# Query softmax of the next block, spread over the steps of a block

## The chip, the cores and the metric

The kernel runs on one core of a Trainium2 chip. The metric is the device time of one execution in microseconds, as the median of several runs. The core has TensorE (PE: matmuls; PEld: its weight loads), VectorE (DVE), ScalarE (ACT), GpSimd (POOL) and SyncE (SP), whose queue issues the DMAs. Each engine works through its own instructions in the order of the program and waits on semaphores for the others.

## What is computed

Attention over 49 agents, and two MLP layers without a residual. All is float32; there are 12480 tokens of 128 channels, and both MLPs have 2048 hidden units.

```python
def sm(a, b):
    s = (1/sqrt(128)) * (a @ b.T)
    s = s - s.max(-1, keepdims=True)
    e = np.exp(s)
    return e / (e.sum(-1, keepdims=True) + 1e-09)

agent_v = sm(agents, k) @ v            # 49 x 128
x = sm(q, agents) @ agent_v            # 12480 x 128
x = np.maximum(x @ w_in1, 0)**2 @ w_out1
h = x @ w_in2
return (np.maximum(h, 0) + alpha * np.minimum(h, 0)) @ w_out2
```

## The kernel before

The first part (up to about 120 us) reads k and v, makes the agents' attention and from it `agent_v`, and multiplies that with the first MLP's input weights once: W1 = agent_v @ w_in1. After that a query's softmax weights are all that the first layer needs. Every operand of these matmuls is split into a high and a low half (`...h`, `...l`), and a product is the sum of three matmuls, so an activation costs not only its ReLU but also a high copy and a subtraction for the low half.

The second part is one loop (line 748) over steps `s`. The 12480 queries are 25 blocks: one of 320 queries, 23 of 512, one of 384. A block is 8 steps (`b, i = divmod(s, 8)`), and a step handles 256 hidden units of both layers, of different blocks:

- `H1(s)`: first layer in, 6 matmuls into the PSUM tile `h1`; ScalarE does the ReLU (L647) and later the square (L757).
- `O(s - 2, ...)`: first layer out, 12 matmuls, from the halves `g1h` and `g1l` of step s - 2.
- `G1(s)`: VectorE makes `g1h` (L658) and `g1l` (L660); in a few steps of the first two blocks ScalarE or GpSimd does one of them.
- `H2(s - 11)`: second layer in, 12 matmuls into the PSUM tile `h2`; ScalarE makes `g2h` by a ReLU (L714), then VectorE makes `g2l` (L715), which reads `h2` too. There is one `h2`, so the next `H2` waits for `g2l`.
- `O2`: second layer out, 12 matmuls, one step behind `H2`.

At the end of a block come extra pieces: `X1_copy`, `X1_add` and `X1` (in step 1 of the next block: the first layer's result, its halves, `xl` on L694) and `OUT` (in step 3: copy on ScalarE, add and 32x32 transpose on VectorE, DMA).

Beside this the loop prepares the softmax of the next block's queries, mostly on VectorE. `q_transpose` (tile `qT`), `q_split_hi` on ScalarE and `q_split_lo` make the query's halves; `q_scores` is 12 narrow matmuls into `s_ps`, in the PSUM tile `h1`; `q_squares` transposes the scores back into the tile `s`. Each of the four groups of 32 partitions holds 25 agents (or 24 and a repeated one), so that two groups share a query. `q_max` reduces over 25, exchanges the results between the two groups (`swap`, four small copies on L282), takes the maximum of both (`m`) and subtracts it. `q_exp` is the exponential on ScalarE. `q_norm` sums, corrects for the repeated agent, exchanges, adds, takes the reciprocal and multiplies. `q_back` transposes back (`e2`, which shares the one buffer of `qT`), and `q_hi` and `q_lo` make the halves `qsh` and `qsl` for the next block's `H1`.

Which step does which is written by hand in two tables (lines 736 and 737). Entries of `before` come ahead of `H1` in a step's program, those of `after` at its end; the engines keep that order. The stretch from H1's first matmul to the next step's is called a step below, and step numbers are `i`.

Of the kernel before, what the change touches and what calls it, by code (L numbers as in the profile page):

```python
# [8 lines left out]
F32 = mybir.dt.float32  # L9
# [10 lines left out]
def agent_attention_moe_kernel(  # L20
# [43 lines left out]
    QB = 32  # L64
    NT = 512

    NQS = [10] + [NT // QB] * 23 + [12]
    assert sum(NQS) * QB == N
    Q0 = [sum(NQS[:b]) for b in range(len(NQS))]
    NB = len(NQS)  # L70
    H = 64
    GA = (NA + 1) // 2
# [13 lines left out]
    qp = ctx.enter_context(tc.tile_pool(name="qp", bufs=2))  # L86
# [82 lines left out]
    with tc.manual_schedule():  # L169
# [51 lines left out]
            return t_.rearrange("p r g a -> p (r g a)")  # L221


        q_sb, qh_sb, ql_sb, s2_ps, t_sb, e_sb, qs_sb = {}, {}, {}, {}, {}, {}, {}

        def flat(t_):
            return t_.rearrange("p j c -> p (j c)")
# [15 lines left out]
        def q_transpose(b):  # L243
            if b >= NB:
                return
            t_ = qp.tile([128, NT], F32, tag="qT", name="qT", bufs=1)[:, :QB * NQS[b]]
            nc.vector.transpose(t_, q_sb[b])
            q_sb[b] = t_

        def q_split_hi(b):  # L250
            if b >= NB:
                return
            qh_sb[b] = qp.tile([128, NT], F32R, tag="qh", name="qh", bufs=1)[:, :QB * NQS[b]]
            nc.scalar.copy(qh_sb[b], q_sb[b])

        def q_split_lo(b):
            if b >= NB:
                return
            ql_sb[b] = qp.tile([128, NT], F32R, tag="ql", name="ql", bufs=1)[:, :QB * NQS[b]]
            nc.vector.tensor_tensor(out=ql_sb[b], in0=q_sb.pop(b), in1=f32(qh_sb[b]), op=ALU.subtract)  # L260
# [17 lines left out]
        def swap(t_):  # L278

            for i in range(4):  # L280
                o = i ^ 1
                nc.vector.tensor_copy(t_[i * QB:(i + 1) * QB, 1, :], t_[o * QB:(o + 1) * QB, 0, :])  # L282
# [12 lines left out]
        def q_max(b):  # L295
            if b >= NB:
                return
            s = t_sb[b][:, :, :GA]
            mx = qp.tile([128, 2, NT // QB], F32, tag="mx", name="mx")[:, :, :NQS[b]]
            nc.vector.tensor_reduce(out=mx[:, 0, :], in_=s, op=ALU.max, axis=AX.X)  # L300
            swap(mx)
            m = qp.tile([128, NT // QB, 1], F32, tag="m", name="m")[:, :NQS[b]]
            nc.vector.tensor_tensor(out=m[:, :, 0], in0=mx[:, 0, :], in1=mx[:, 1, :], op=ALU.max)
            nc.vector.tensor_tensor(out=s, in0=s, in1=m.to_broadcast([128, NQS[b], GA]), op=ALU.subtract)  # L304

        def q_exp(b):
# [2 lines left out]
            s = t_sb[b][:, :, :GA]  # L309
            nc.scalar.activation(s, s, AF.Exp, scale=SCALE)  # L310

        def q_norm(b):
            if b >= NB:
                return
            s = t_sb[b][:, :, :GA]
            sm = qp.tile([128, 2, NT // QB], F32, tag="sm", name="sm")[:, :, :NQS[b]]
            nc.vector.tensor_reduce(out=sm[:, 0, :], in_=s, op=ALU.add, axis=AX.X)

            nc.vector.scalar_tensor_tensor(
                out=sm[:, 0, :], in0=s[:, :, GA - 1], scalar=notpad, in1=sm[:, 0, :], op0=ALU.mult, op1=ALU.add  # L320
            )
            swap(sm)
            r = qp.tile([128, NT // QB, 1], F32, tag="r", name="r")[:, :NQS[b]]
            nc.vector.scalar_tensor_tensor(
                out=r[:, :, 0], in0=sm[:, 0, :], scalar=1e-9, in1=sm[:, 1, :], op0=ALU.add, op1=ALU.add
            )
            nc.vector.reciprocal(r, r)
            nc.vector.tensor_tensor(out=s, in0=s, in1=r.to_broadcast([128, NQS[b], GA]), op=ALU.mult)  # L328

        def q_back(b):  # L330
            if b >= NB:
                return

            e = qp.tile([128, NT], F32, tag="qT", name="e2", bufs=1)[:, :QB * NQS[b]]
            nc.vector.transpose(e, flat(t_sb.pop(b)))
            e_sb[b] = e

# [79 lines left out]
        def m_add(g):  # L417
            p_ = mP.pop(g)
            if g == 0:
                nc.scalar.copy(Mf, p_[:, :C])  # L420
            else:
                nc.vector.tensor_tensor(out=Mf, in0=Mf, in1=p_[:, :C], op=ALU.add)
            if g == 3:
                nc.vector.tensor_copy(Mh, Mf)
                nc.vector.tensor_tensor(out=Ml, in0=Mf, in1=f32(Mh), op=ALU.subtract)


        with tc.tile_pool(name="att", bufs=1) as att:
# [67 lines left out]
            def at(plan, c):  # L496
                for x in plan.get(c, "").split():
                    name, g = x[1:4], int(x[5:])
                    if x[0] == "+":
                        w_begin(name, g)  # L500
                    elif name == "wi1":
                        w_conv(name, g, wi1[:, g * QW:(g + 1) * QW])
                    else:
                        w_split(name, g)
# [75 lines left out]
            def exp_chunk(c):  # L580
                d = s_all[:, c * KC:(c + 1) * KC, :]
                nc.vector.tensor_tensor(out=d, in0=d, in1=gbc.to_broadcast([P, KC, NA]), op=ALU.subtract)
                nc.scalar.activation(d, d, AF.Exp, scale=SCALE)
                e1_sb[c] = d

            def av_chunk(c):
                e, t_ = e1_sb.pop(c), chunk("v", c)
                for j in range(KC):
                    mm(av_ps, e[:, j, :], t_[:, j, :],
                       start=(c == 0 and j == 0), stop=(c == NKC - 1 and j == KC - 1))  # L590
                done["ring"] += 1
                pump()
# [3 lines left out]
            q_transpose(0)  # L596
            q_split_hi(0)
            q_split_lo(0)
            q_steps = {0: q_scores, 1: q_squares, 2: q_max, 3: q_exp, 5: q_norm, 6: q_back, 7: q_hi, 9: q_lo}
            for c in range(NKC):  # L600
                if c + 2 < NKC:
                    exp_chunk(c + 2)
                av_chunk(c)
                if c in q_steps:
                    q_steps[c](0)
                at(v_plan, c)

            rinv = att.tile([NA, 1], F32, name="rinv")
# [28 lines left out]
        def H1(s):  # L637
            b, i = divmod(s, NP)
            n = width(b)
            p_ = ps("h1", "h1_ps")[:, :, :n]  # L640
            qh, ql = qs_sb[b]
            mm2(
                lambda r: p_[:, r],
                [lambda r, w=w, x=x: (w[rows(r), i], x[rows(r)]) for w, x in ((W1l, qh), (W1h, ql), (W1h, qh))],
            )
            g = wk.tile([128, 2, NT], F32, tag="g1", name="g1")[:, :, :n]
            nc.scalar.activation(g, p_, AF.Relu)  # L647
            h1g[s] = g
# [31 lines left out]
        def X1_copy(b):  # L680
            x = xp.tile([128, NT], F32, tag="x", name="x", bufs=1)[:, :width(b)]
            nc.scalar.copy(x, o1p[b][:, 0])
            x1[b] = x
# [49 lines left out]
                nc.sync.dma_start(out=ov[i][:, Q0[b]:Q0[b] + NQS[b]], in_=ot[i * QB:(i + 1) * QB])  # L733


        before = {0: q_transpose, 1: q_split_lo, 4: q_max, 5: q_norm, 6: q_back, 7: q_lo}
        after = {0: q_split_hi, 4: q_exp, 6: q_hi}

        def m_finish(g):
            m_product(g)  # L740
            m_add(g)

        pend = []
        M_STEP = 11

# [1 line left out]
        LO_ON_POOL = (0, 3, 4, 6, 7, 9, 10, 11, 15)  # L747
        for s in range(S + D + 2):
            b, i = divmod(s, NP)
            if i in before:  # L750
                before[i](b + 1)
            if s < S:
                H1(s)
            if 0 <= s - LAG1 < S:
                O(s - LAG1, h1g, wo1h, wo1l, o1p, "o1")
            if s < S:
                nc.scalar.activation(h1g[s], h1g[s], AF.Square)  # L757
            bx, ix = divmod(s - LAG1, NP)
            ends = ix == NP - 1 and 0 <= bx < NB
            if ends:  # L760
                X1_copy(bx)

            if i == 1:
                q_scores(b + 1)
                q_squares(b + 1)
            for f, t in ((m_transpose, M_STEP + 1), (m_finish, M_STEP + 2)):
                if 0 <= s - t < 8 and (s - t) % 2 == 0:
                    f((s - t) // 2)
            if ends:
                X1_add(bx)  # L770
            if s < S:
                G1(s)
            if 0 <= s - D < S:
                H2(s - D)
                pend.append(s - D)
            if ends:
                X1(bx)
            while pend and len(pend) > (LAG2 if s < S else 2) or pend and s >= S + D:
                O2(pend.pop(0))
            for bo in sorted(outp):  # L780
                OUT(bo)
            if i in after:
                after[i](b + 1)
            if i == 0:
                q_load(b + 3)
            at(s_plan, s)
            if 10 <= s < 14:
                m_scale(s - 10)
            if 0 <= s - M_STEP < 8 and (s - M_STEP) % 2 == 0:
                m_join((s - M_STEP) // 2)  # L790
# [30 lines left out]
```

## Time and profile before

| What | Value |
|---|---|
| Median of 3 runs (lowest, highest) | 1174.03 us (1173.48, 1174.31) |
| The profiled execution, and its span | 1174.41 us, 1172.6 us |
| Busy in the span: PE, DVE, ACT, POOL | 1116.7, 909.4, 737.7, 75.4 us |
| Chain that ended last: PE, DVE, ACT | 58%, 31%, 5% |
| Mean granted clock of TensorE | 0.954 |

The profile is one execution. The span runs from the first to the last instruction; the execution's own time is a little longer. Busy time is summed by engine, so 95% of TensorE is a mean over a start in which it waits and a long regular part in which it hardly does. The chain of work that ended last is followed back from the end: at each step to what released the instruction, or to the one before it on its engine.

### The profile page before, as it was taken

To read this page: it belongs to the slowest core of one execution; us is meant where nothing else is said; L and a number is where in the kernel's file an instruction comes from. 1 tells how busy PE (TensorE), PEld (TensorE's weight loads), DVE (VectorE), ACT (ScalarE), POOL (GpSimd) and SP (SyncE) were. 2 spreads that over 40 slices of the span, in tenths; PEclk is the share of its full clock that TensorE was granted. 3 is DMA by queue.
4 is the path that set the end of the run, shared out by engine and by line. 5 is a ranking of instruction groups with operands and counts; after the bars stand their busy time and mean duration, and the time that the engine had idled before them with its cause. 6 is when DMAs were issued, how large, how long until landed. Compare 5 with 4: busy or idle time off the path is not lost.

```text
span 1172.6 us, 22345 instructions
## 1 busy us (share of the span) xinstructions
PE 1116.7 (95%) x9463; PEld 910.2 (78%) x9463; DVE 909.4 (78%) x1355; ACT 737.7 (63%) x846; POOL 75.4 (6%) x56
## 2 busy tenths in 40 slices
PE   8986779999999999999999999999999999999997
PEld 7975568878778777877877787787777778778886
DVE  3478786887888788788888878888887887888753
ACT  3334666667667666766666666666666666666642
POOL 2037441000000000000000000000000000000000
PEclk6568889999999999999999999999999999999999
DMA  9996011011111111111110111111011111001010
GB/s 200 196 200 153 11 21 28 16 28 33 21 22 37 28 18 29 28 19 28 37 29 15 32 28 20 28 37 24 15 37 28 19 27 35 12 17 28 19 24 17
DMA packets 145283, 48.22 MB, mean 41 GB/s; under 512 B 107101, under 2 KB 138782, under 8 KB 145182
## 3 DMA queue, kind: packets, MB, share of 16 engines
q1 hardware_dynamic: 145182, 46.79, 20.2%
q8 instruction: 74, 1.21, 0.4%
q14 instruction: 27, 0.22, 0.1%
HBM read 27.59 MB, written 6.39 MB: 29 GB/s over the span
## 4 chain that ended last, share of the span: by engine, by line
PE 58%; DVE 31%; ACT 5%; issue 2%; POOL 1%; DMA 1%; SPq 0%; DVEq 0%; POOLq 0%
PE o L90 27%; PE h_ps L90 23%; DVE g1l L660 7%; DVE g2l L715 6%; PE s_ps L90 5%; DVE g1h L658 4%; ACT g L647 2%; ACT g L757 2%; PE kT_ps L475 2%; DVE sm L282 2%; DVE mx L282 1%; DVE ot L731 1%; DVE o L729 1%; DVE s L328 1%; DVE s L304 1%
## 5 line engine op out<-in xcount | busy, mean ns | idle before, releaser
L714 ACT ACTIVATE g2h<-h_ps 128x1024 fp32r<-128x1024 f32 (+2 forms) x200 | 201.6, 1008 | 174.3 <-PE h_ps L90 153.9
L647 ACT ACTIVATE g<-h_ps 128x1024 f32<-128x1024 f32 (+2 forms) x200 | 201.2, 1006 | 151.7 <-PE h_ps L90 147.5
L715 DVE SCALAR_TENSOR_TENSOR g2l<-h_ps,g2h 128x1024 fp32r<-128x1024 f32 (+2 forms) x200 | 238.4, 1192 | 30.6 <-ACT g2h L714 30.4
L660 DVE TENSOR_TENSOR g1l<-g,g1h 128x1024 fp32r<-128x1024 f32 (+2 forms) x191 | 230.7, 1208 | 6.5
L658 DVE CAST g1h<-g 128x1024 fp32r<-128x1024 f32 (+2 forms) x198 | 137.2, 693 | 124.6 <-ACT g L757 123.5
L757 ACT ACTIVATE g<-g 128x1024 f32<-128x1024 f32 (+2 forms) x200 | 207.8, 1039 | 6.3
L90 PE MATMUL o<-g1l,wo1h 64*128 64x512 f32 (+2 forms) x800 | 157.7, 390 | 1.1 <-POOL g1l L660 0.7
L90 PE MATMUL o<-g2l,wo2h 64*128 64x512 f32 (+2 forms) x800 | 157.6, 388 | 0.6 <-DVE g2l L715 0.6
L90 PE MATMUL o<-g1h,wo1l 64*128 64x512 f32 (+2 forms) x800 | 157.2, 389 | 0.7 <-DVE g1h L658 0.7
L90 PE MATMUL o<-g2h,wo2l 64*128 64x512 f32 (+2 forms) x800 | 157.8, 388 | 0.0
L90 PE MATMUL o<-g1h,wo1h 64*128 64x512 f32 (+2 forms) x800 | 157.6, 390 | 0.0
L90 PE MATMUL o<-g2h,wo2h 64*128 64x512 f32 (+2 forms) x800 | 157.2, 387 | 0.0
L90 PE MATMUL h_ps<-xh,wi2l 64*128 64x512 f32 (+2 forms) x400 | 83.1, 410 | 9.0 <-DVE g2l L715 8.9
L90 PEld LDWEIGHTS o<-g1l,wo1h 64*128 64x128 f32 x800 | 76.4, 187 | 19.0 <-POOL g1l L660 1.6
L90 PEld LDWEIGHTS o<-g1h,wo1l 64*128 64x128 f32 x800 | 76.6, 188 | 17.9 <-DVE g1h L658 1.0
L90 PEld LDWEIGHTS o<-g2l,wo2h 64*128 64x128 f32 x800 | 76.8, 186 | 17.2 <-DVE g2l L715 0.8
L90 PEld LDWEIGHTS o<-g2h,wo2h 64*128 64x128 f32 x800 | 76.8, 186 | 16.6
L90 PEld LDWEIGHTS o<-g2h,wo2l 64*128 64x128 f32 x800 | 76.7, 186 | 16.4 <-ACT g2h L714 0.2
L90 PEld LDWEIGHTS o<-g1h,wo1h 64*128 64x128 f32 x800 | 76.4, 187 | 16.4
L90 PE MATMUL h_ps<-qsh,W1l 64*128 64x512 f32 (+2 forms) x400 | 79.7, 395 | 5.0 <-ACT g L647 2.7
L90 PE MATMUL h_ps<-sl,wi2h 64*128 64x512 f32 (+2 forms) x400 | 79.2, 388 | 0.4 <-DMA sl<-xl 0.4
L90 PE MATMUL h_ps<-qsl,W1h 64*128 64x512 f32 (+2 forms) x400 | 79.1, 392 | 0.5 <-DVE qsl L350 0.5
(144 smaller groups left out, 1623.8 us busy)
## 6 DMA issues: line engine op xcount, KB each, us to landing
ring<-in_k_dram SPq DMA_DIRECT2D x13, 480.0 KB, 10.7
ring<-in_v_dram SPq DMA_DIRECT2D x13, 480.0 KB, 9.0
q_sb<-in_q_dram SPq DMA_DIRECT2D x184, 32.0 KB, 1.8
sh<-xh SPq DMA_DIRECT2D x46, 128.0 KB, 2.3
sl<-xl SPq DMA_DIRECT2D x46, 128.0 KB, 2.3
out_dram<-ot SPq DMA_DIRECT2D x92, 64.0 KB, 1.9
raw<-in_moe_w_out_dram SPq DMA_DIRECT2D x8, 512.0 KB, 6.0
raw<-in_moe_w_in_dram SPq DMA_DIRECT2D x4, 512.0 KB, 10.4
```

Source lines behind the costliest of these rows:

```text
L90: nc.tensor.matmul(o, lhsT, rhs, start=start, stop=stop)
L282: nc.vector.tensor_copy(t_[i * QB:(i + 1) * QB, 1, :], t_[o * QB:(o + 1) * QB, 0, :])
L304: nc.vector.tensor_tensor(out=s, in0=s, in1=m.to_broadcast([128, NQS[b], GA]), op=ALU.subtract)
L328: nc.vector.tensor_tensor(out=s, in0=s, in1=r.to_broadcast([128, NQS[b], GA]), op=ALU.mult)
L475: nc.tensor.transpose(p_[:, j // TB, (j % TB) * P:(j % TB + 1) * P], t_[:, j, :C], ident[:P, :P])
L647: nc.scalar.activation(g, p_, AF.Relu)
L658: nc.vector.tensor_copy(gh, g)
L660: eng.tensor_tensor(out=gl, in0=g, in1=f32(gh), op=ALU.subtract)
L714: nc.scalar.activation(gh, p_, AF.Relu)
L715: nc.vector.scalar_tensor_tensor(out=gl, in0=p_, scalar=0.0, in1=f32(gh), op0=ALU.max, op1=ALU.subtract)
L729: nc.vector.tensor_tensor(out=x, in0=x, in1=p_[:, 1], op=ALU.add)
L757: nc.scalar.activation(h1g[s], h1g[s], AF.Square)
```

## The change

`q_max` is cut in two (`q_max` up to `m`, `q_sub`), and so is `q_norm` (`q_sum` up to the exchange, `q_norm` from there). The tables get new steps: maximum in 2, subtraction in 3 with the exponential at its end, sum in 4, norm in 5. `q_transpose` and `q_split_hi` move from step 0 to the end of the block before that (step 7, `ahead` 2); for block 1 they stand in front of the loop. `q_split_lo` moves from step 1 to step 0. `qT` and `e2` get two buffers. The first block's softmax, in the agents' part, keeps its steps.

```diff
@@ q_transpose
-            t_ = qp.tile([128, NT], F32, tag="qT", name="qT", bufs=1)[:, :QB * NQS[b]]
+            t_ = qp.tile([128, NT], F32, tag="qT", name="qT", bufs=2)[:, :QB * NQS[b]]
@@ q_max
             nc.vector.tensor_tensor(out=m[:, :, 0], in0=mx[:, 0, :], in1=mx[:, 1, :], op=ALU.max)
+            m_sb[b] = m
+
+        def q_sub(b):
...
+            m = m_sb.pop(b)
             nc.vector.tensor_tensor(out=s, in0=s, in1=m.to_broadcast([128, NQS[b], GA]), op=ALU.subtract)
@@ q_norm
-        def q_norm(b):
+        def q_sum(b):
...
             swap(sm)
+            m_sb[b] = sm
+
+        def q_norm(b):
...
+            sm = m_sb.pop(b)
@@ q_back
-            e = qp.tile([128, NT], F32, tag="qT", name="e2", bufs=1)[:, :QB * NQS[b]]
+            e = qp.tile([128, NT], F32, tag="qT", name="e2", bufs=2)[:, :QB * NQS[b]]
@@ the tables
-        before = {0: q_transpose, 1: q_split_lo, 4: q_max, 5: q_norm, 6: q_back, 7: q_lo}
-        after = {0: q_split_hi, 4: q_exp, 6: q_hi}
+        before = {
+            0: [(q_split_lo, 1)], 2: [(q_max, 1)], 3: [(q_sub, 1)], 4: [(q_sum, 1)], 5: [(q_norm, 1)],
+            6: [(q_back, 1)], 7: [(q_lo, 1), (q_transpose, 2)],
+        }
+        after = {3: [(q_exp, 1)], 6: [(q_hi, 1)], 7: [(q_split_hi, 2)]}
...
+        q_transpose(1)
+        q_split_hi(1)
@@ the loop
-            if i in before:
-                before[i](b + 1)
+            for f, ahead in before.get(i, ()):
+                f(b + ahead)
```

VectorE before the change, from step 4 of a block into step 5 (`mx`, `m`, `sm`, `r` belong to the softmax; `g1h`, `g1l`, `g2l` are the regular three):

```order
L300 TENSOR_REDUCE mx<-s_2835 128x16
L282 COPY mx<-mx 32x16 x4
L303 TENSOR_TENSOR m<-mx 128x16
L304 TENSOR_TENSOR s_2835<-s_2835,m 128x16x25
L658 CAST g1h<-g_3018 128x1024
L660 TENSOR_TENSOR g1l<-g_3018,g1h 128x1024
L715 SCALAR_TENSOR_TENSOR g2l<-h_ps,g2h 128x1024
L317 TENSOR_REDUCE sm<-s_2835 128x16
L319 SCALAR_TENSOR_TENSOR sm<-s_2835,notpad,sm 128x16
L282 COPY sm<-sm 32x16 x4
L324 SCALAR_TENSOR_TENSOR r<-sm 128x16
L327 RECIPROCAL r<-r 128x16
```

The maximum and the subtraction stand in front of one step's regular three, the sum and the norm together behind them, in front of the next step's.

VectorE after, the end of step 1 to the start of step 4 of the block that follows:

```order
L710 TENSOR_TENSOR xl<-x,xh 128x512
L300 TENSOR_REDUCE mx<-s_3363 128x16
L282 COPY mx<-mx 32x16 x4
L303 TENSOR_TENSOR m<-mx 128x16
L674 CAST g1h<-g_3425 128x1024
L676 TENSOR_TENSOR g1l<-g_3425,g1h 128x1024
L731 SCALAR_TENSOR_TENSOR g2l<-h_ps,g2h 128x1024
L311 TENSOR_TENSOR s_3363<-s_3363,m 128x16x25
L674 CAST g1h<-g_3482 128x1024
L676 TENSOR_TENSOR g1l<-g_3482,g1h 128x1024
L731 SCALAR_TENSOR_TENSOR g2l<-h_ps,g2h 128x1024
```

The maximum now stands behind `xl` in step 2, the subtraction alone in step 3.

VectorE after, steps 4 and 5:

```order
L324 TENSOR_REDUCE sm<-s_2835 128x16
L326 SCALAR_TENSOR_TENSOR sm<-s_2835,notpad,sm 128x16
L282 COPY sm<-sm 32x16 x4
L674 CAST g1h<-g_3026 128x1024
L676 TENSOR_TENSOR g1l<-g_3026,g1h 128x1024
L731 SCALAR_TENSOR_TENSOR g2l<-h_ps,g2h 128x1024
L338 SCALAR_TENSOR_TENSOR r<-sm 128x16
L341 RECIPROCAL r<-r 128x16
L342 TENSOR_TENSOR s_2835<-s_2835,r 128x16x25
L674 CAST g1h<-g_3092 128x1024
L676 TENSOR_TENSOR g1l<-g_3092,g1h 128x1024
L731 SCALAR_TENSOR_TENSOR g2l<-h_ps,g2h 128x1024
```

The sum follows the output's two instructions, and the regular three stand between it and the norm.

ScalarE before, the end of step 3 to step 5 (`o` is the output's copy, `s` the exponential):

```order
L728 COPY o<-o_4638 128x512
L647 ACTIVATE g_5130<-h_ps 128x1024
L757 ACTIVATE g_5130<-g_5130 128x1024
L714 ACTIVATE g2h<-h_ps 128x1024
L310 ACTIVATE s_4947<-s_4947 128x16x25
L647 ACTIVATE g_5204<-h_ps 128x1024
L757 ACTIVATE g_5204<-g_5204 128x1024
```

ScalarE after, the same place:

```order
L744 COPY o<-o_4646 128x512
L317 ACTIVATE s_4947<-s_4947 128x16x25
L663 ACTIVATE g_5138<-h_ps 128x1024
L779 ACTIVATE g_5138<-g_5138 128x1024
L730 ACTIVATE g2h<-h_ps 128x1024
L663 ACTIVATE g_5204<-h_ps 128x1024
L779 ACTIVATE g_5204<-g_5204 128x1024
```

The exponential has moved from behind step 4's `g2h` to in front of step 4's ReLU, right behind the output's copy.

## Rows read from the trace of the kernel before

**Rows 1.** Busy time by stretch: us, then PE, PEld, DVE, ACT, POOL, PEclk, DMA
```profile
core 0 of [0], span 1172.6 us
...
119.00:222.00 103.00, 85.80 (x780) 70.89 (x780) 82.12 (x129) 67.22 (x91) 32.15 (x20) 0.90 0.10 19
222.00:1100.00 878.00, 869.02 (x7534) 693.18 (x7534) 722.08 (x1058) 594.23 (x638) 0.00 (x0) 1.00 0.13 26
```

**Rows 2.** Waits from 222 to 1100 us: total us, times, longest
```profile
PEld h_ps L90 <- DVE g2l L715: 23.1, 41, 0.9
PE h_ps L90 <- DVE g2l L715: 8.9, 20, 0.5
```

**Rows 3.** Timeline of TensorE, one block: start, us, engine, line, operation
```profile
402.63 0.40 PE L90 MATMUL h_ps<-qsh,W1l 64*128 64x512 f32 x2
...
409.63 0.40 PE L90 MATMUL h_ps<-xh,wi2l 64*128 64x512 f32 x2
...
412.43 0.40 PE L90 MATMUL h_ps<-qsh,W1l 64*128 64x512 f32 x2
...
418.02 0.39 PE L90 MATMUL h_ps<-qsh,W1l 64*128 64x512 f32 x2
...
420.12 0.46 PE L90 MATMUL h_ps<-xh,wi2l 64*128 64x512 f32 x2
...
422.97 0.39 PE L90 MATMUL h_ps<-qsh,W1l 64*128 64x512 f32 x2
...
425.67 0.50 PE L90 MATMUL h_ps<-xh,wi2l 64*128 64x512 f32 x2 [0.45 <-DVE g2l L715]
...
428.57 0.39 PE L90 MATMUL h_ps<-qsh,W1l 64*128 64x512 f32 x2
```

**Rows 4.** Timeline of VectorE, the same block
```profile
400.04 0.78 DVE L292 STREAM_TRANSPOSE s<-s_ps 128x256 f32<-128x256 f32 x2 [1.17 <-PE s_ps L90]
...
404.30 0.68 DVE L694 TENSOR_TENSOR xl<-x,xh 128x512 fp32r<-128x512 f32 x1
...
414.94 0.53 DVE L300 TENSOR_REDUCE mx<-s 128x16 f32<-128x400 f32 x1
415.50 0.70 DVE L282 COPY mx<-mx 32x16 f32<-32x16 f32 x4
...
416.45 0.58 DVE L304 TENSOR_TENSOR s<-s,m 128x400 f32<-128x400 f32 x1
...
418.80 1.22 DVE L715 SCALAR_TENSOR_TENSOR g2l<-h_ps,g2h 128x1024 fp32r<-128x1024 f32 x1
...
419.94 0.56 DVE L317 TENSOR_REDUCE sm<-s 128x16 f32<-128x400 f32 x1
...
421.55 0.17 DVE L324 SCALAR_TENSOR_TENSOR r<-sm 128x16 f32<-128x16 f32 x1
...
422.54 0.69 DVE L658 CAST g1h<-g 128x1024 fp32r<-128x1024 f32 x1
...
424.40 1.22 DVE L715 SCALAR_TENSOR_TENSOR g2l<-h_ps,g2h 128x1024 fp32r<-128x1024 f32 x1
```

**Rows 5.** Timeline of ScalarE, the same block
```profile
412.63 0.59 ACT L728 COPY o<-o 128x512 f32<-128x512 f32 x1 [0.37 <-PE o L90]
...
413.33 1.03 ACT L647 ACTIVATE g<-h_ps 128x1024 f32<-128x1024 f32 x1
...
417.06 0.56 ACT L310 ACTIVATE s<-s 128x400 f32<-128x400 f32 x1
```

**Rows 6.** Timelines of three engines, the first two blocks
```profile
121.79 0.60 ACT L254 CAST qh<-qT 128x512 fp32r<-128x512 f32 x1
...
149.58 0.58 PE L90 MATMUL s_ps<-ql,agTh 64*128 64x256 f32 x2 [1.60 <-DVE ql L260]
...
161.68 5.21 DVE L282 COPY mx<-mx 32x16 f32<-32x16 f32 x4
...
165.91 0.51 PE L406 MATMUL wT_ps<-ident,wf 64*128 64x64 f32 x8 [4.53 <-POOL wf L398]
```

More of the change, by code (lines that the diff above doesn't have):

```diff
@@ L221, in cols @@
             return t_.rearrange("p r g a -> p (r g a)")
-        q_sb, qh_sb, ql_sb, s2_ps, t_sb, e_sb, qs_sb = {}, {}, {}, {}, {}, {}, {}
+        q_sb, qh_sb, ql_sb, s2_ps, t_sb, m_sb, e_sb, qs_sb = {}, {}, {}, {}, {}, {}, {}, {}
         def flat(t_):
@@ L303, in q_max @@
             nc.vector.tensor_tensor(out=m[:, :, 0], in0=mx[:, 0, :], in1=mx[:, 1, :], op=ALU.max)
+            m_sb[b] = m
+        def q_sub(b):
+            if b >= NB:
+                return
+            s = t_sb[b][:, :, :GA]
+            m = m_sb.pop(b)
             nc.vector.tensor_tensor(out=s, in0=s, in1=m.to_broadcast([128, NQS[b], GA]), op=ALU.subtract)
@@ L322, in q_norm @@
             swap(sm)
+            m_sb[b] = sm
+        def q_norm(b):
+            if b >= NB:
+                return
+            s = t_sb[b][:, :, :GA]
+            sm = m_sb.pop(b)
             r = qp.tile([128, NT // QB, 1], F32, tag="r", name="r")[:, :NQS[b]]
@@ L598, in agent_attention_moe_kernel @@
             q_split_lo(0)
-            q_steps = {0: q_scores, 1: q_squares, 2: q_max, 3: q_exp, 5: q_norm, 6: q_back, 7: q_hi, 9: q_lo}
+            q_steps = {
+                0: [q_scores], 1: [q_squares], 2: [q_max, q_sub], 3: [q_exp], 5: [q_sum, q_norm], 6: [q_back], 7: [q_hi], 9: [q_lo]
+            }
             for c in range(NKC):
@@ L603, in agent_attention_moe_kernel @@
                 av_chunk(c)
-                if c in q_steps:
-                    q_steps[c](0)
+                for f in q_steps.get(c, ()):
+                    f(0)
                 at(v_plan, c)
@@ L733, in OUT @@
                 nc.sync.dma_start(out=ov[i][:, Q0[b]:Q0[b] + NQS[b]], in_=ot[i * QB:(i + 1) * QB])
-        before = {0: q_transpose, 1: q_split_lo, 4: q_max, 5: q_norm, 6: q_back, 7: q_lo}
-        after = {0: q_split_hi, 4: q_exp, 6: q_hi}
+        before = {
+            0: [(q_split_lo, 1)], 2: [(q_max, 1)], 3: [(q_sub, 1)], 4: [(q_sum, 1)], 5: [(q_norm, 1)],
+            6: [(q_back, 1)], 7: [(q_lo, 1), (q_transpose, 2)],
+        }
+        after = {3: [(q_exp, 1)], 6: [(q_hi, 1)], 7: [(q_split_hi, 2)]}
         def m_finish(g):
@@ L781, in agent_attention_moe_kernel @@
                 OUT(bo)
-            if i in after:
-                after[i](b + 1)
+            for f, ahead in after.get(i, ()):
+                f(b + ahead)
             if i == 0:
```

## Prediction

> **What bounds the kernel now.** I read the busy time by stretch first. Between 222 and 1100 us, three quarters of the 1172.6 us span, TensorE is busy 869.02 of 878.00 us at a granted clock of 1.00 (2.4 GHz), VectorE 722.08 and GpSimd 0.00 [rows 1]. TensorE is the bound there, and at most what it stands still can be won. Before that, from 119 to 222 us, it is busy 85.80 of 103.00 us at a mean clock of 0.90 [rows 1], so the start is bound by something else.
>
> Then the waits of the same stretch: TensorE waits for one thing only, VectorE's `g2l`, the low half of the second layer's activations. 20 times its matmuls wait, 41 times its weight loads [rows 2]. 20 is once per block of queries. The 8.9 us in that row is too small a measure of the loss, since the records of busy matmuls stretch over part of the wait, so I take the loss from the pace. Two undisturbed steps, 2 and 3 of a block, run from 402.63 to 412.43: 9.80 us, 4.90 each. Steps 5 and 6 of the same block have the same matmuls and run from 418.02 to 428.57: 10.55 us [rows 3]. So a block loses 0.75 us there. The place: the second layer's first matmul stands 2.10 us behind the first layer's (409.63 against 402.63 + 4.90), so in step 6 it was due at 418.02 + 4.90 + 2.10 = 425.02; it came at 425.67, and its record is 0.50 long where others are 0.40 [rows 3].
>
> The timeline of VectorE shows why. In every step it does `g1h` and `g1l` (424.40 - 422.54 = 1.86 us) and `g2l` (419.94 - 418.80 = 1.14 to the next start), 3.00 of the 4.90 us. It has 1.90 us to spare in a step. Step 4 adds the maximum (414.94 to 416.45, 1.51 us) and the subtraction (418.80 - 416.45 - 1.86 = 0.49), step 5 the sum (419.94 to 421.55, 1.61) and the norm (421.55 to 422.54, 0.99) [rows 4]. That is 4.60 us in two steps that have 3.80 free, and step 4 starts late already, behind the output's add and transpose of step 3. VectorE runs without a pause from 414.94; `g2l` of step 4 ends at 418.80 + 1.22 = 420.02, just ahead of step 5's matmul at 420.12, and `g2l` of step 5 at 424.40 + 1.22 = 425.62, right before step 6's late matmul at 425.67 [rows 3, 4]. The second layer's hidden buffer in PSUM exists once, so that matmul cannot start before the last step's `g2l` has read it.
>
> **The change part by part.** No instruction is added or removed on any engine; they change places.
>
> Steps 4 and 5 lose the maximum, the subtraction and the early part of the softmax. Step 4 now starts with the sum: 414.94 + 1.61 + 1.86 + 1.22 = 419.63, against 420.12. That is 0.49 early where it was 0.10. Step 5 has the norm, 0.99 of 1.90 us free. So the stall of step 6 goes whole, 0.75 us. Next late there is TensorE's own pace.
>
> Step 2 receives the maximum, and this is the place to watch. Step 1 cannot move: its two transposes of the scores wait for TensorE (1.17 us idle before 400.04), and behind them come the block's residual add, the three regular instructions and `xl`, which ends at 404.30 + 0.68 = 404.98 [rows 4]. The maximum then ends at 406.49, `g2l` starts at 408.35 and ends at 409.57. TensorE wants the buffer at 409.63 [rows 3]. The margin is 0.06 us. The case of before with a like margin is the matmul of step 5: with `g2l` 0.10 us early that step lasted from 418.02 to 422.97, 4.95 instead of 4.90 [rows 3]. I take that 0.05 us per block as the new cost; ends: 0, since the instruction behind the maximum no longer depends on it, and 0.25, a late weight load and a wait.
>
> Step 3 has the subtraction (0.49) before and the output's add and transpose behind the regular three: free. Step 6 has the transpose back and step 7 the low half and the transpose of the block after next, each of the 128x512 size whose subtraction takes 0.68 [rows 4]: 1.4 us in step 7, under 1.90. In step 0 only the low half of the raw query is left, 0.68. All three lie in VectorE's pause before `g1h`. The transpose is earlier by a step, so its 128x512 buffer must live beside that of the transpose back; with two buffers neither waits for the other. The query load on SyncE's queue waits for that transpose to free its buffer and so becomes free earlier; nothing on that queue waits longer.
>
> On ScalarE the exponential moves from step 4 to the end of step 3, behind the copy of the output. That copy ends at 412.63 + 0.59 = 413.22, the exponential takes 0.56, so the ReLU that started at 413.33 starts at 413.78, 0.45 late [rows 5]. Its square then ends 0.45 later, but `g1h` of step 4 stands behind the sum until 416.55 anyway. Who waits for ScalarE there: TensorE's next first-layer matmul, at 418.02 [rows 3], over 3 us after that ReLU's end at 414.81. Cost nothing; without that cover 0.45 per block.
>
> The start, by bounds. The high half of block 1's query (0.60 us on ScalarE) now stands ahead of the first ReLU, where it stood one step later, and waits for its transpose: I take +0.7 us. For block 2, the transpose comes a step earlier, and the wait of the score matmuls for its low half (1.60 us at 149.58) should go: -1.6. Behind it the longest wait, 4.53 us at 165.91, is for GpSimd's join of weights [rows 6], which is fed by a `g1h` that the maximum now precedes by up to 1.51 us. I take the sum of the start as -1 us, with ends of +4 and -5: less than half of the 17.2 us that TensorE is idle there [rows 1] can reasonably move.
>
> At the start four copies of the maximum took 5.21 us [rows 6] where in the steady part four take 0.70 [rows 4]; GpSimd was at work beside them. The Trainium skill (SBUF — State Buffer, section "Who interferes with whom") says that VectorE's copies and its instructions with two SBUF inputs share a port pair with GpSimd and block whole, and that reductions do not. By that rule spreading the softmax does not help at the start: the sum's copies now meet the GpSimd burst instead of the maximum's. The trace agrees that copies suffer. By the rule the start would be worth up to 4.5 us less, the time about 1163.5; by the rows VectorE is not what TensorE waits for at 165.91, and the sum stays.
>
> **Sum.** 20 blocks x 0.75 = 15.0, less 20 x 0.05 = 1.0, gives -14.0; the start -1. The profiled execution took 1174.41 us, 1.81 around its span, so 1159.4. It stands 0.38 above the median of the runs, 1174.03, so I predict 1159.0.
>
> **The rivals.** (a) Step 2 becomes the stall in part. For: the margin is 0.06 us and the weight load wants the buffer 0.23 earlier still (a step is 21 pairs of matmuls, 4.90 / 21). Against: step 5 of before had nearly the same margin and lost 0.05. With 0.3 us per block: 20 x 0.25 = 5 us less gain, 1164.
>
> (b) The start turns against it: GpSimd's join comes later by the maximum (1.5 us), the first ReLU costs its 0.7 and the wait at 149.58 stays. That is about +3 instead of -1: 1163.
>
> (c) The change does not do what it says: the stall is not VectorE's queue but something that moves with it, and 0.75 us stays. Then 1174. Against it, `g2l` starts in step 5 right when `g1l` ends, with no pause named in its row, and TensorE's row names it as releaser [rows 3, 4].
>
> (d) Slower: the place is step 2. Everything VectorE does from 400.04 on hangs from TensorE's scores, and each 0.1 us beyond the margin costs 20 x 0.1 = 2 us, so from 0.9 us per block on the kernel is slower than before. If the copies of the maximum ran there as at the start, 5.21 instead of 0.70, the block would lose 4.4 us and the kernel take about 1247. Against it: GpSimd does nothing in those blocks [rows 1]. A smaller slowing of the reduction or of the copies would end in (a).
>
> **How the numbers follow.** Forecast 75%, (a) 9%, (b) 7%, (c) 5%, (d) 4%. The time is the forecast's. The range runs from 1154 (no new cost in step 2, start -5) to 1166 (a and b together nearly); (c) and (d) are left out, with a little of each tail. A median of three tells 0.2%, 2.3 us, from no change: faster 0.91 (forecast, a, b), within 0.2% 0.05, slower 0.04.
>
> **What would show it.** Right: steps 5 and 6 of a block take 9.80 us, the matmul waits for `g2l` all but vanish, TensorE's chain has little of VectorE left in the steady part, and a block of 512 queries is shorter by 0.7 us; the largest remaining wait is the weight load in front of step 3's second layer. Wrong: a TensorE wait for `g2l` at step 3 of each block as long as the old one, a ReLU of step 4 that TensorE waits for, or a start that is longer by more than 4 us at the point where the blocks become regular.

## The result and the profile after

| | Before | After |
|---|---|---|
| Median of 4 runs (lowest, highest) | 1173.76 us (1172.72, 1174.31) | 1156.85 us (1155.9, 1159.55) |
| The profiled execution, its span | 1174.41, 1172.6 us | 1155.9, 1154.1 us |

The ratio is 0.9861, interval 0.9843 to 0.9879: faster by 16.9 us, where 15.0 were forecast.

The chain of work that ended last, by engine, from the page of the kernel after:

```profile
PE 90%; DVE 4%; DMA 2%; ACT 1%; POOL 1%; issue 1%; SPq 0%; POOLq 0%; DVEq 0%; ACTq 0%
```

TensorE had 58% of it before and VectorE 31%; VectorE is down to 4%. Busy time by stretch, with the columns of [rows 1]:

```profile
119.00:222.00 103.00, 86.03 (x780) 71.67 (x782) 82.72 (x128) 66.72 (x90) 32.44 (x20) 0.87 0.10 19
222.00:1080.00 858.00, 858.00 (x7506) 693.76 (x7504) 718.79 (x1057) 589.61 (x636) 0.00 (x0) 1.00 0.13 26
```

By its records TensorE is busy without a gap from 222 to 1080 us; the start from 119 to 222 us looks as before, with a lower mean clock (0.87 for 0.90). The waits of the steady part (222 to 1085 us: total us, times, longest) answer to [rows 2]:

```profile
DVE s L292 <- PE s_ps L90: 36.7, 21, 1.8
...
PEld s_ps L90 <- ACT g L663: 3.4, 21, 0.2
...
PEld h_ps L90 <- DVE g2l L731: 0.6, 4, 0.2
```

No matmul waits for `g2l` any more. The largest wait left to TensorE is a weight load of the scores, 0.2 us each time, with no matmul waiting behind it; the same row, 3.4 us, stood in the waits before. The first row is slack, and it has grown (before 24.4 us, 1.2 at the longest): VectorE is earlier at the scores. The timeline of TensorE, a block that answers to [rows 3], with the starts of steps 2, 4, 5, 6 and 7 and three first matmuls of the second layer:

```profile
399.14 0.40 PE L90 MATMUL h_ps<-qsh,W1l 64*128 64x512 f32 x2
...
406.14 0.39 PE L90 MATMUL h_ps<-xh,wi2l 64*128 64x512 f32 x2
...
408.93 0.39 PE L90 MATMUL h_ps<-qsh,W1l 64*128 64x512 f32 x2
...
414.51 0.39 PE L90 MATMUL h_ps<-qsh,W1l 64*128 64x512 f32 x2
...
416.60 0.39 PE L90 MATMUL h_ps<-xh,wi2l 64*128 64x512 f32 x2
...
419.39 0.39 PE L90 MATMUL h_ps<-qsh,W1l 64*128 64x512 f32 x2
...
421.48 0.39 PE L90 MATMUL h_ps<-xh,wi2l 64*128 64x512 f32 x2
...
424.27 0.39 PE L90 MATMUL h_ps<-qsh,W1l 64*128 64x512 f32 x2
```

Steps 5 and 6 take 424.27 - 414.51 = 9.76 us where they took 10.55, and the second layer comes 2.09 us behind the first in step 6 as in step 5. VectorE in the same block answers to [rows 4]:

```profile
396.55 0.78 DVE L292 STREAM_TRANSPOSE s<-s_ps 128x256 f32<-128x256 f32 x2 [1.74 <-PE s_ps L90]
...
400.81 0.68 DVE L710 TENSOR_TENSOR xl<-x,xh 128x512 fp32r<-128x512 f32 x1
401.41 0.56 DVE L300 TENSOR_REDUCE mx<-s 128x16 f32<-128x400 f32 x1
...
402.75 0.18 DVE L303 TENSOR_TENSOR m<-mx 128x16 f32<-128x16 f32 x1
402.84 0.69 DVE L674 CAST g1h<-g 128x1024 fp32r<-128x1024 f32 x1
...
404.70 1.22 DVE L731 SCALAR_TENSOR_TENSOR g2l<-h_ps,g2h 128x1024 fp32r<-128x1024 f32 x1
...
414.89 1.22 DVE L731 SCALAR_TENSOR_TENSOR g2l<-h_ps,g2h 128x1024 fp32r<-128x1024 f32 x1
...
417.56 0.69 DVE L674 CAST g1h<-g 128x1024 fp32r<-128x1024 f32 x1 [0.47 <-ACT g L779]
...
419.43 1.22 DVE L731 SCALAR_TENSOR_TENSOR g2l<-h_ps,g2h 128x1024 fp32r<-128x1024 f32 x1
```

Three ends of `g2l` against three matmuls of TensorE: 404.70 + 1.22 = 405.92 against 406.14 (0.22 early), 416.11 against 416.60 (0.49), 420.65 against 421.48 (0.83). And VectorE waits again, 0.47 us ahead of `g1h` in step 5: the backlog that ran through steps 4 and 5 is gone.

**Where the 18.5 us between the two spans lie.** I compare the starts of the same matmul in both traces. The loop begins at 118.85 instead of 119.66 (-0.81; that work is the same, and over the ten traces of this study its end lies between 117.1 and 121.9). From there to the start of block 3 the kernel after takes 107.95 instead of 107.28 (+0.67). Blocks 3 to 23 take 850.21 instead of 867.05 (-16.84). Block 24 up to its last first-layer step takes 32.07 in both. The tail behind that takes 45.03 instead of 46.56 (-1.53). Together -18.5.

The length of each step, from H1's first matmul to the next one's, as a mean over blocks 3 to 22:

| Step | 0 | 1 | 2 | 3 | 4 | 5 | 6 | 7 | block |
|---|---|---|---|---|---|---|---|---|---|
| Before | 4.887 | 5.599 | 4.897 | 4.891 | 5.584 | 4.959 | 5.603 | 4.892 | 41.312 |
| After | 4.885 | 5.595 | 4.888 | 4.889 | 5.576 | 4.883 | 4.885 | 4.883 | 40.485 |

Steps 1 and 4 are long in both, so only steps 5 and 6 were stalled. They give back 0.794 of the 0.827 us per block.

### The profile page after: what moved, and what is told of

Its sections match the earlier page's. It is cut to its first block, busy times and chain, and to the rows that moved or that the text cites. A ratio compares the mean times of both kernels' runs of the same rounds, so it can differ in the third digit from the quotient of the medians.

```text
span 1154.1 us, 22343 instructions
## 1 busy us (share of the span) xinstructions
PE 1107.5 (96%) x9463; PEld 912.7 (79%) x9463; DVE 909.6 (79%) x1355; ACT 734.7 (64%) x846; POOL 75.8 (7%) x56
## 4 chain that ended last, share of the span: by engine, by line
PE 90%; DVE 4%; DMA 2%; ACT 1%; POOL 1%; issue 1%; SPq 0%; POOLq 0%; DVEq 0%; ACTq 0%
PE o L90 48%; PE h_ps L90 35%; PE s_ps L90 5%; PE kT_ps L489 2%; DMA ring<-in_k_dram 1%; POOL g1l L676 1%; DVE s_all L596 1%; DMA ring<-in_v_dram 0%; DVE bits L155 0%; DMA raw<-in_moe_w_out_dram 0%; PE M_ps L90 0%; DVE g1h L674 0%; PE av_ps L90 0%; DVE bits L158 0%; DVE bits L152 0%
## 5 line engine op out<-in xcount | busy, mean ns | idle before, releaser
L676 DVE TENSOR_TENSOR g1l<-g,g1h 128x1024 fp32r<-128x1024 f32 (+2 forms) x191 | 233.3, 1222 | 6.9 <-ACT g1h L672 0.4
L90 PEld LDWEIGHTS o<-g1h,wo1l 64*128 64x128 f32 x800 | 76.7, 188 | 16.9
L90 PE MATMUL h_ps<-sh,wi2l 64*128 64x512 f32 (+2 forms) x400 | 79.2, 388 | 0.3 <-DMA sh<-xh 0.2
```

Source lines behind the costliest of these rows:

```text
L90: nc.tensor.matmul(o, lhsT, rhs, start=start, stop=stop)
L676: eng.tensor_tensor(out=gl, in0=g, in1=f32(gh), op=ALU.subtract)
```

## The experiments

The theories, by the letters that the expectations use. **Q**: the stall is a backlog of VectorE's in-order queue, summed over steps 4 and 5 against the due time of `g2l`. Against it stood **P**, that the place of a piece decides rather than the sum; **M**, that the moved transposes and splits bring part of the gain; **B**, that VectorE's total work sets the pace; **S**, that a late step is made good in the next. For the start: **F**, that the first ReLU behind `q_split_hi` is what the start loses, and **G**, that the start ends with GpSimd's join, whatever comes ahead of it.

**The maximum alone.** Before's kernel with `q_max` cut in two, and one piece moved:

```diff
-before = {0: q_transpose, 1: q_split_lo, 4: q_max, 5: q_norm, 6: q_back, 7: q_lo}
+before = {0: [q_transpose], 1: [q_split_lo], 2: [q_max], 4: [q_sub],
+          5: [q_norm], 6: [q_back], 7: [q_lo]}
```

> The kernel before with one edit: the maximum moves to step 2; subtraction and exponential stay in step 4, sum and norm together in step 5, the query's transpose and halves where they were. Theory Q (queue sum: g2l of step 5 is late by what VectorE has queued over both steps): step 5's g2l ends 414.94 + 0.49 + 1.86 + 1.14 + 2.60 + 1.86 + 1.22 - waits = about 424.2, 0.8 us ahead of the matmul due at 425.02; the stall goes whole, about 15 to 16 us, 1158 to 1159. Rival P (place: the 2.6 us right in front of step 5's regular three make the stall): 1174. Rival M (the moved transpose and halves bring part of the gain): 1161 to 1164.

Measured: 1159.67 us against 1174.39, ratio 0.9871 (0.9856 to 0.9886), 0.7 above the expected range. A block takes 40.496 us, after's length within 0.011. `g2l` of step 5 and the matmul of step 6 that it must precede, from two timelines (VectorE, TensorE) of this kernel:

```profile
422.26 1.22 DVE L726 SCALAR_TENSOR_TENSOR g2l<-h_ps,g2h 128x1024 fp32r<-128x1024 f32 x1
```

```profile
424.29 0.39 PE L90 MATMUL h_ps<-xh,wi2l 64*128 64x512 f32 x2
```

It ends at 423.48, 0.81 us early, as Q's sum said (0.8). This one move brings the whole steady gain, though the sum and the norm still stand together in front of step 5's regular three, so P falls. The rest of the change adds nothing there. In the traces this kernel is 2.1 us longer than after's from the loop's start to block 3 (110.02 against 107.95) and 1.6 longer in the tail.

**The norm alone.** Before's kernel with `q_norm` cut in two; the maximum and the subtraction stay in step 4, the sum in 5, and the norm goes into step 6:

```diff
+before = {0: [q_transpose], 1: [q_split_lo], 4: [q_max], 5: [q_sum],
+          6: [q_norm, q_back], 7: [q_lo]}
```

> The kernel before with the other edit: only the norm (add, reciprocal, multiply) moves, to step 6; maximum and subtraction stay in step 4, the sum in step 5. Theory Q: step 5's g2l ends 419.94 + 1.61 + 1.86 + 1.22 = 424.63, 0.39 ahead of 425.02, weight load just covered; step 5's matmul stays as close as before (0.05 us). Stall gone but for that: 1158 to 1160. Rival P: the same. Rival M: 1161 to 1164.

Measured: 1160.18 us, ratio 0.9879 (0.9864 to 0.9893), 0.2 above the expected range. VectorE's two `g2l` and, below, the matmuls of steps 5 and 6 that they must precede:

```profile
419.22 1.22 DVE L726 SCALAR_TENSOR_TENSOR g2l<-h_ps,g2h 128x1024 fp32r<-128x1024 f32 x1
...
423.83 1.22 DVE L726 SCALAR_TENSOR_TENSOR g2l<-h_ps,g2h 128x1024 fp32r<-128x1024 f32 x1
```

```profile
420.53 0.47 PE L90 MATMUL h_ps<-xh,wi2l 64*128 64x512 f32 x2
...
425.48 0.40 PE L90 MATMUL h_ps<-xh,wi2l 64*128 64x512 f32 x2
```

In step 6 `g2l` is 425.48 - 425.05 = 0.43 early, and the step is clean. In step 5 it is 0.09 early, and the price of so narrow a margin is paid as before: step 5 takes 4.974 and a block 40.607. The maximum took 1.51 us out of the backlog's beginning, the norm 0.99 out of its end [rows 4]; either is more than the 425.62 - 425.02 = 0.60 us that was missing. 0.99 - 0.60 = 0.39 was to be the margin in step 6, and 0.43 is. That speaks for Q: a sum with a due time, and no one piece in it is the culprit.

**The transposes alone.** After's kernel with the softmax pieces back in steps 4 and 5, so that only `q_transpose`, `q_split_hi` and `q_split_lo` stay moved:

```diff
-    0: [(q_split_lo, 1)], 2: [(q_max, 1)], 3: [(q_sub, 1)], 4: [(q_sum, 1)], 5: [(q_norm, 1)],
+    0: [(q_split_lo, 1)], 4: [(q_max, 1), (q_sub, 1)], 5: [(q_sum, 1), (q_norm, 1)],
-after = {3: [(q_exp, 1)], 6: [(q_hi, 1)], 7: [(q_split_hi, 2)]}
+after = {4: [(q_exp, 1)], 6: [(q_hi, 1)], 7: [(q_split_hi, 2)]}
```

> The changed kernel with the softmax put back (maximum and subtraction in step 4, sum and norm in step 5); only the query's transpose and halves are moved. Theory Q: the stall of 0.75 us stays in every block, the start loses under 2 us: 1173 to 1176. Rival M: 3 to 5 us faster than before, 1169 to 1171.

Measured: 1173.99 us (10 runs), ratio 0.9994 (0.9984 to 1.0005); a block of 41.297. Its waits in the steady part are those of [rows 2]:

```profile
PEld h_ps L90 <- DVE g2l L731: 22.6, 40, 0.9
PE h_ps L90 <- DVE g2l L731: 8.9, 20, 0.5
```

M falls: this part of the change moves nothing that can be measured in a block or in the time.

**Four copies more in step 2.** After's kernel, the exchange of the maximum done twice:

```diff
             swap(mx)
+            swap(mx)
```

> The changed kernel with the four exchange copies of the maximum done twice in step 2 (0.74 us more of VectorE per block; the result is the same). Theory Q: in step 2 g2l ended 405.92 against a matmul at 406.14, so 0.22 us are free; the rest, 0.52 us and about 0.1 at the first matmul, is lost in each of 21 blocks: 12 to 13 us, 1168 to 1171. Rival B (the bound is VectorE's total work): 23 x 0.74 = 17 us, 1174. Rival S (a late step is made good later in the block): 1157 to 1160.

Measured: 1177.07 us (10 runs), ratio 1.0018 (1.0008 to 1.0029): the whole gain is lost, and a little more. Its waits from 240 to 1080 us, then VectorE and TensorE at one step 3:

```profile
PEld h_ps L90 <- DVE g2l L732: 20.5, 21, 1.0
PE h_ps L90 <- DVE g2l L732: 11.3, 21, 0.6
```

```profile
408.48 1.54 DVE L282 COPY mx<-mx 32x16 f32<-32x16 f32 x8
...
412.02 1.22 DVE L732 SCALAR_TENSOR_TENSOR g2l<-h_ps,g2h 128x1024 fp32r<-128x1024 f32 x1
```

```profile
410.49 0.39 PE L90 MATMUL h_ps<-qsh,W1l 64*128 64x512 f32 x2
...
413.29 0.50 PE L90 MATMUL h_ps<-xh,wi2l 64*128 64x512 f32 x2 [0.55 <-DVE g2l L732]
```

The old stall, made anew in step 3: the same two waits, the same 0.50 record. `g2l` ends at 413.24, the matmul was due at 410.49 + 2.10 = 412.59, so it is 0.65 late. Step 3 becomes 5.705 instead of 4.889, every other step stays clean, and a block takes 41.326. The stall and its place are Q's, the size was expected too small, 12 to 13 us where 18 to 20 came (2.7 over before, and after 14.9 to 16.9 under it). Two terms were wrong: the copies cost 0.83 us (1.54 against 0.71), and 0.65 us late costs not 0.65 but 0.82 in the step (20 x 0.84 per block = 16.8). Some 2 us more lie at the start (109.84 us from the loop's start to block 3, after 107.95), and those are not shown to be the copies': the kernel with the maximum alone took 110.02 there. S falls: no later step makes anything good.

**The same four copies in step 6.** After's kernel, with the exchange repeated at the start of `q_back`:

```diff
         def q_back(b):
             if b >= NB:
                 return
+            swap(mx_sb.pop(b))
```

> The changed kernel with the same four copies a second time in step 6 instead of step 2, ahead of the transpose back. Theory Q: step 6 has 1.90 us free and uses 0.62; 0.74 more stays in VectorE's pause: no change, 1156 to 1158. Rival B (VectorE's total work): 17 us slower, 1174.

Measured: 1159.8 us, ratio 0.989 (0.9873 to 0.9907); after's kernel, run once more beside it (1156 to 1158 were expected), took 1157.89 (1154.38 to 1158.24), ratio 0.9872 (0.9855 to 0.9889). The intervals overlap, but the time lies 1.8 above Q's range. In the traces blocks 3 to 23 hold 0.7 of the difference (850.98 against 850.27); the start holds 2.7 (110.72 against 108.03), 0.7 of it ahead of the first step that has the copies. Its block is 40.528 against 40.490, and one row of its waits is all that is left of `g2l`:

```profile
PEld h_ps L90 <- DVE g2l L734: 0.5, 3, 0.2
```

Steps 6 and 7 take 4.887 and 4.883, as in after's kernel. The 0.04 lies in step 1 (5.638 against 5.593), and the kernel start_late below, which has no added copies, has it there too (5.641). So 0.8 us of VectorE's time cost 0.84 us per block in step 2 and nothing that can be seen in step 6. B falls: it is not how much VectorE does but when.

**The start, later and earlier.** After's kernel, once with the two splits of block 1 where before has them (behind step 0 and in step 1), and once with its transpose and high half ahead of the agents' part's end:

```diff
 start_late:
-        q_split_hi(1)
 ...
+            if s == 1:
+                q_split_lo(1)
             for f, ahead in before.get(i, ()):
-                f(b + ahead)
+                if s > 0:
+                    f(b + ahead)
 ...
+            if s == 0:
+                q_split_hi(1)
 start_early:
+            q_transpose(1)
+            q_split_hi(1)
             rinv = att.tile([NA, 1], F32, name="rinv")
 ...
-        q_transpose(1)
-        q_split_hi(1)
```

> The changed kernel with the high half of block 1's query back behind step 0, its low half back in step 1, as in the kernel before. Theory F (the first ReLU waits behind that high half, TensorE stands 2 us and its clock falls to the lower level): 1 to 2 us faster than the changed kernel, 1155 to 1156. Rival G (the start ends with GpSimd's join of weights, which comes when it comes): no change, 1156.5 to 1157.5.

> The changed kernel with the transpose and the high half of block 1's query moved to where VectorE and ScalarE wait for TensorE, before the attention's result is scaled. Theory F: neither stands in front of the first ReLU nor behind it: 1.5 to 2.7 us faster, 1154 to 1155.5. Rival G: no change, 1156.5 to 1157.5.

Measured: 1156.47 us (1155.26 to 1157.32) and 1156.26 (1156.1 to 1156.88), ratios 0.9858 (0.9842 to 0.9874) and 0.9858 (0.9844 to 0.9873). Their medians lie 1.4 and 1.6 us under the 1157.89 of after's kernel beside them, the size that F forecast, but that kernel's four runs spread over 3.9 us and the intervals overlap: neither can be told from it. What F speaks of is there, in after's ScalarE and TensorE at the loop's start:

```profile
120.30 0.62 ACT L254 CAST qh<-qT 128x512 fp32r<-128x512 f32 x1 [1.37 <-DVE qT L247]
```

```profile
121.58 0.64 PE L90 MATMUL h_ps<-qsh,W1l 64*128 64x320 f32 x2 [2.01 <-ACT g L663]
...
165.88 0.69 PE L420 MATMUL wT_ps<-ident,wf 64*128 64x64 f32 x8 [4.53 <-POOL wf L412]
```

With the pieces earlier the wait of the first ReLU shrinks, but the wait for the join stays as it was, in start_early's kernel:

```profile
120.65 0.42 PE L90 MATMUL h_ps<-qsh,W1l 64*128 64x320 f32 x2 [0.80 <-ACT g L665]
...
164.42 0.69 PE L420 MATMUL wT_ps<-ident,wf 64*128 64x64 f32 x8 [4.56 <-POOL wf L412]
```

From the loop's start the join comes after 46.25 us before, 47.03 after, 45.69 with the pieces late and 45.28 with them early. So in these traces 1.75 us are won up to the join with the pieces early, against G. But then TensorE's clock takes most of it back. Two stretches right behind the wait, in start_early and then in after, with the columns of [rows 1]:

```profile
164.42:167.83 3.41, 3.41 (x30) 3.41 (x32) 3.00 (x3) 2.23 (x3) 3.18 (x3) 0.50 0.02 5
167.83:171.24 3.41, 3.41 (x24) 2.50 (x20) 2.50 (x5) 1.41 (x2) 0.00 (x0) 0.68 0.00 0
```

```profile
165.88:168.72 2.84, 2.83 (x26) 2.84 (x28) 2.43 (x3) 1.93 (x3) 2.84 (x3) 0.50 0.03 6
168.72:171.56 2.84, 2.84 (x28) 2.15 (x24) 2.77 (x5) 1.50 (x3) 0.35 (x1) 0.95 0.00 0
```

Behind the join the granted clock stays longer at the lower of its two levels, 1.2 GHz, in the earlier kernel: the same stretch of work takes 6.82 us instead of 5.68. In both kernels the clock fell while TensorE stood still ahead of the join, 3.7 us before the join's end in after (162.16) and 1.2 before it in start_early (163.21); it rose 3.1 and 5.6 us behind it. From the loop's start to block 3 there remain 107.60 us (early), 107.55 (late) and 107.95 (after). So F was right on the wait, and of the time that it forecast 0.35 to 0.40 us reach block 3 in these traces, which G's "no change" describes better. No version among these beats the changed kernel measurably.

## Why the prediction was right, by its steps

- **The stall of steps 5 and 6 goes whole, 0.75 us.** Right: 0.794 in the two steps. `g2l` of step 4 is 0.49 us early, as the sum gave; that of step 5 0.83, as the room in step 5 let expect. The small difference is the undisturbed pace: 4.885 us as a mean, where I had read 4.90 from one pair of steps.
- **The new cost in step 2, 0.05 us.** Wrong in size: 0. The margin is 0.22 us, not 0.06. I let the maximum start when `xl` ends (0.68), while it starts 401.41 - 400.81 = 0.60 behind its start; and I kept 1.51 us from the maximum to what follows, as in [rows 4], where the subtraction needs `m`. Now `g1h` follows, which doesn't: 402.84 - 401.41 = 1.43. That is 0.16 together. The sign named for a right forecast, that the largest remaining wait would be the weight load in front of step 3's second layer, was nearly right. Its row of waits has only the 4 longest, but that weight load stands still for 0.11 to 0.16 us in each of blocks 3 to 22. In the block shown it starts at 405.98, 0.06 behind the end of `g2l` at 405.92, where the weight load ahead of it ended at 405.86. It costs the step nothing (4.889 us). The weight load of the scores, 0.2 us, waits a little longer.
- **The steady part, -14.0 us.** Right in kind, 2.8 too small: 20 x 0.827 = 16.5 and 0.3 in block 23 make the 16.84. Of the 2.8, 1.0 is the cost in step 2 that did not come; the rest is the block's 0.827 for 0.75, and block 23. That the time still came within 2 us of the forecast owes something to luck: the start, put at -1, gave +0.67 and so took back 1.7 of the 2.8.
- **The exponential on ScalarE costs nothing.** Right. Copy, exponential and ReLU of step 4 in after's timeline answer to [rows 5]:

```profile
409.14 0.59 ACT L744 COPY o<-o 128x512 f32<-128x512 f32 x1 [0.37 <-PE o L90]
409.62 0.56 ACT L317 ACTIVATE s<-s 128x400 f32<-128x400 f32 x1
410.07 1.02 ACT L663 ACTIVATE g<-h_ps 128x1024 f32<-128x1024 f32 x1
```

The ReLU stands 1.14 us behind the step's start at 408.93, before 0.90. It is 0.24 later, not 0.45, and step 4 is no longer for it.
- **The start, -1 us.** Wrong in sign by a little: +0.67 from the loop's start to block 3. The wait for block 2's low half did go; the scores' step is 1.78 us shorter for it (forecast 1.6). But the first ReLU made TensorE wait 2.01 us (shown above) instead of 0.80, since ScalarE's cast waits 1.37 for the transpose, and TensorE then ran at the lower clock level from 121.2 to 131.4 us; two steps into the loop the kernel stood 1.97 us later, where I had put 0.7. The same wait before:

```profile
121.16 0.41 PE L90 MATMUL h_ps<-qsh,W1l 64*128 64x320 f32 x2 [0.80 <-ACT g L647]
```

The two nearly cancel, within the range of +4 to -5; and since this stretch takes between 107.3 and 110.7 us over the ten traces, the sign of 0.67 is not settled by one trace of before. As for the rule on ports that the prediction took up: in after's VectorE at the start, with GpSimd at work, the sum's pieces are

```profile
161.07 0.55 DVE L324 TENSOR_REDUCE sm<-s 128x16 f32<-128x400 f32 x1
161.65 1.99 DVE L326 SCALAR_TENSOR_TENSOR sm<-s,notpad,sm 128x16 f32<-128x16 f32 x1
163.68 4.18 DVE L282 COPY sm<-sm 32x16 f32<-32x16 f32 x4
```

In the steady part the last two take 0.24 and 0.70 us, the reduction 0.53. The Trainium skill (SBUF — State Buffer, section "Who interferes with whom") says just this: a reduction never contends with GpSimd, copies and instructions with two SBUF inputs can. The trace agrees on which instructions grow, and the loss did move from the maximum's copies to the sum's. What was worked out from it, 4.5 us at the start, did not come: the join's wait is 4.53 us as in [rows 6], and the join stands 0.78 us later from the loop's start, for the first ReLU's sake at least in part.
- **The tail** was not in the sum: -1.53 us, and not the change's. Two stretches of 4 us near the end, before and after, each behind the same wait for a DMA (`sh` and `sl`):

```profile
1142.00:1146.00 4.00, 3.85 (x21) 3.59 (x23) 0.10 (x1) 0.00 (x0) 0.00 (x0) 0.57 0.02 4
```

```profile
1125.00:1129.00 4.00, 3.83 (x35) 3.57 (x37) 0.78 (x2) 0.81 (x1) 0.00 (x0) 1.00 0.02 5
```

TensorE's clock fell to the lower level in the first and not in the second. Over the ten profiles the tail takes either 45.0 or 46.6 us: in all five of 46.6 the clock falls 16 to 18 us into the tail and rises again, in the five of 45.0 it falls only within the last 5 us. Before's kernel with the maximum alone takes 46.6, with the norm alone 45.0, and after's with the copies in step 6 takes 46.6.

**The rivals.** (a), a new stall in step 2, did not come; the run with four more copies shows what lies beyond the margin of 0.22 us. (b), the start against it, holds in sign in these two traces (+0.67, not +3; its own two terms, 1.5 and 0.7, add up to 2.2), and the sign is not settled. (c), that the stall is not VectorE's queue, fell with the two runs that each move one piece. (d), slower by way of step 2, names the right place: 0.83 us more on VectorE there lost 0.84 us per block, and blocks 3 to 23 then take as long as before (867.54 us against 867.05). So the kernel breaks even at about 0.83 per block, the gain itself; the prediction's own terms give (15.0 + 1) / 20 = 0.8, not its 0.9. The 2.7 us by which that run is slower than before lie mostly in the start (109.84 against 107.28), which is not shown to be the copies'. (d)'s price, 0.1 us lost for each 0.1 beyond the margin, was too low: 0.65 late cost 0.82.

What stays open: why the clock fell 1.2 us before the join's end in start_early and 3.7 before it in after, with almost the same wait ahead of it; and which of the start's shifts is due to the sum's slow copies. The same stretch from the loop's start to block 3 took 107.95 and 108.03 us in two traces of the same kernel, and from 109.8 to 110.7 in four others that differ little from it or from before, so shifts of under 3 us there are not explained here.

## What to carry to other kernels

Where an engine in order feeds a matmul at fixed times, don't ask how busy it is (VectorE was 82% busy before and 84% after in the steady part) but add up its queue over the steps from its last pause and hold it against each due time; here either of two pieces, each larger than the missing time, cured a backlog over two steps when it was taken out. Give the steps into which pieces move the same sum: here 0.22 us were left in step 2, while step 6 swallowed 0.8. What was won here ahead of a long wait of TensorE's was mostly lost behind it at the lower clock level: read the granted clock behind such a wait before counting the gain.

## What the runs showed of the hardware

- Where a second-layer matmul waited for its buffer in PSUM, the step grew by more than the lateness, and in two kernels by the same amount more. As means over blocks 3 to 22, against the step's own start + 2.10 us: 0.55 late made step 6 longer by 0.72 before, 0.66 late made step 3 longer by 0.82 with the copies, some 0.16 more each time. The matmul starts 0.05 us after the instruction that releases it ends, and its record is 0.50 long instead of 0.39. (The 0.60 used further up counts from a clean step 5.)
- A narrow margin costs a little as well: with `g2l` some 0.08 us early as a mean, step 5 was 0.07 us longer before and 0.09 with the norm alone; with 0.20 early, step 3 of the changed kernel was not longer (4.889).
- VectorE's next instruction starts 0.09 us behind the start of the 0.18 us `m` where it is `g1h`, which doesn't need `m`, and 0.21 behind where it is the subtraction, which does; so it is in every block of the steady part, in three traces each. The second case, in before:

```profile
416.24 0.18 DVE L303 TENSOR_TENSOR m<-mx 128x16 f32<-128x16 f32 x1
```

- Eight small copies in a row take 1.54 us, four 0.71.
- The granted clock goes with tails of 45.0 or 46.6 us in the ten traces, whose tails have the same instructions: behind the same wait 21 matmuls ran in 4 us at a mean of 0.57, 35 at 1.00.
